# Top-k attention and two MLPs on one core: scores kept in PSUM, the mask on ScalarE, and another spread of the weight preparation

## The chip, the cores and the metric

The kernel runs on one core of one Trainium2 chip. The metric is the device time in microseconds (us) of one launch; lower is better. The engines are TensorE (PE, with its weight loads as PEld), VectorE (DVE), ScalarE (ACT), GpSimd (POOL) and SyncE (SP), which here issues all DMAs.

## What is computed

The reference chains an attention that keeps the 32 largest scores of each row and two MLPs of 512 x 2048 x 512 over 2304 tokens (4 batches x 576):

```python
scores = scale * np.matmul(q, k.transpose(0, 1, 3, 2))          # 4 batches, 8 heads, 576 x 576
kth = np.partition(scores, -32, axis=-1)[..., -32:-31]
scores = np.where(scores >= kth, scores, -1e9)
attn = softmax(scores)                                          # with 1e-9 in the denominator
x = np.matmul(attn, v)                                          # -> 2304 x 512
h = x @ w_in1;  g = where(h >= 1, h, where(h <= -1, 0, (h + 1) ** 2 / 4));  x = g @ w_out1
h = np.maximum(x @ w_in2, 0);  out = (h * h) @ w_out2
```

All arrays are float32. The kernel computes matrix products with pairs of float16: every operand is split into a high part and a low part (the rest), and three products (high x high, high x low, low x high) are added in PSUM.

## The kernel before

**Tiles and slots.** 2304 tokens are 18 token tiles of 128. One *tile* of the attention (number t, 144 in all) is one token tile and one head: 128 rows of 576 scores. Two of the token tiles, 4 and 13, straddle two batches; their scores and attends take twice as many matmuls of half the rows. One *MLP group* is a token tile and a quarter of the 2048 hidden columns, 12 matmuls for the input product and 12 for the output product, all 512 columns wide; there are 72 groups of each MLP, 144 in all.

**A tile of the attention.** PE makes the scores with four matmuls (512 and 64 columns, two parts) in a PSUM tile `s` (`scores`, L782). ACT copies them to an SBUF tile `S` (`scores_copy`, L795), of which there are five. DVE finds the 32 largest with four `max` (eight values each) and, between them, three `match_replace`, which overwrite the values found (`topk_ops`, L802); the first `max` and the first `match_replace` read `S`, the others the work tile `W`. A `match_replace` shows in the trace as two rows, MATCH_VALUE_LOAD and MATCH_REPLACE8. POOL makes the bias of the exponential (`exp_bias`), ACT takes the exponential of `S` (`exp`), DVE multiplies it with the comparison of `S` to the 32nd value (`mask`, a scalar_tensor_tensor). ACT writes the high part over `S` (`prob_hi`), POOL the low part in two pieces (`prob_lo`), SP issues a DMA transpose to `pT`, and PE multiplies with the values in 14 matmuls (`attend`, into `acc`).

**An MLP group.** PE fills `h` in PSUM (two banks). For the first MLP (`m == 1`) ACT makes two relus of `h` with different scales, POOL clamps the first (tensor_scalar to `r`), ACT squares it, POOL adds the second (tensor_tensor to `r`). For the second MLP ACT makes a relu and a square. ACT and POOL then split the result into `g`, SP transposes it to `gT`, and PE multiplies with the output weights into `o` (`mlp_act` to `mlp_out`). `y_finish` normalises the first MLP's result: its `hl_y<-o,sy,hl_y` on DVE reads PSUM.

**Weights.** The four weights come as float32, 16 slices of 128 x 512 each; they lie in the SBUF tile `wall`. `w_decode` (ACT, POOL and DVE, the last a scalar_tensor_tensor over 512 elements) brings the loaded words into a scaled form, `w_norm` sums squares on PE, `w_scale` makes a scale, and `w_split` (L512) makes high and low parts: for the first MLP with a float32 matmul by a diagonal, whose result ACT copies, for the second on ACT and POOL.

**The order.** Functions are noted at steps (eight steps are one slot of one tile) that the table `PLAN` sets. A planner, `Book.order`, puts the noted operations into one order per engine by a list schedule: every operation has a cost from `Book.costs`, an operation that is ready runs where its engine is free, the smaller key first. The engines then run that order as it stands. DVE's `max` operations form a beat; other operations may run at most 12 of them ahead.

Of the kernel before, what the change touches and what calls it, by code (L numbers as in the profile page):

```python
# [16 lines left out]
P = 128  # L17
# [4 lines left out]
TOPK = 32  # L22
# [13 lines left out]
    soon=dict(s=8, att=8, a=8, x=24),  # L36
    kch=(0, 0, 0, 1), vch=(0, 0, 1), scale=(0, 1, 2, 3, 4, 5), dch=(0, 1, 3), qch=(0, 0, 3, 4), k0=(-5, -4, -2),
    d0=(-8, -6, -4, -2), l0=(-9, -6), n0=(0, 1, 0, 1, 2, 3), q01=-5, v0l=-2, v0n=(5, 7, 9, 11), v0s=14, vn=60, vnd=7,
    vnl=18, vs=241, meet=248, mc1=252, m2c0=121, m2c1=265, v0=(21, 25, 29, 33, 37, 41, 45, 49), kv1=(254, 10, 289, 6),
# [107 lines left out]
class Book:  # L147
# [3 lines left out]
    def __init__(self, nc):  # L151
# [3 lines left out]
        self.shift = 0  # L155

    def tile(self, pool, bufs, shape, dtype, tag, name, given):
        ring = self.rings.get((id(pool), tag))
        if ring is None:
            ring = self.rings[id(pool), tag] = Ring(pool, bufs, dict(tag=tag, **given))  # L160
# [4 lines left out]
    def pool(self, real, bufs):  # L165
        book = self

        class Pool:
            def tile(self, shape, dtype, tag, name, **given):
                return book.tile(real, given.get("bufs", bufs), shape, dtype, tag, name, given)  # L170
# [12 lines left out]
    def note(self, engine, method, fn, args, kwargs):  # L183
# [7 lines left out]
        deps = set()  # L191
# [11 lines left out]
        for v in ins:  # L203
            c = v.cover()
            deps.update(n for d, n in v.tile.writes if meet(c, d))
            v.tile.reads.append((c, op.n))
        for v in outs:
# [14 lines left out]
            t.writes.append((c, op.n))  # L222
        op.load = method == "dma_start"
# [1120 lines left out]
```

## Time and profile before

| what | value |
|---|---|
| three runs, median | 1165.53 us (1162.1 to 1168.16) |
| profiled execution, its own time | 1160.56 us |
| its span, first to last instruction | 1158.8 us |
| busy: PE, DVE, ACT, POOL | 1000.6, 985.1, 855.3, 833.6 us |
| mean granted clock of PE | 0.975 |

All sums below are made against the profiled execution. The page of the profile gives busy shares; `out<-in` in a row names the tile that is written and those that are read. Nearly every row carries the line L339, since the planner emits all operations there, so rows are told apart by tile names: `m` holds the maxima, `s` and `S` scores, `W` the work tile and the probabilities, `r`, `g`, `h`, `o` belong to the MLP, `wall` to the weights. Matmuls are pipelined and their ends are modelled, so for PE the distance from start to start is the measure.

### The profile page before, as it was taken

Reading aid. Unit: us, or ns where it says so; the run is one execution under the profiler, and the core shown is the slowest. Engines: PE = TensorE matmul, PEld = TensorE weight load, DVE = VectorE, ACT = ScalarE, POOL = GpSimd, SP = SyncE. Lnnn points to the kernel's source line nnn. Section 1 sums busy time; section 2 is a strip of 40 time slices with the busy share of each in tenths; the row PEclk is TensorE's granted clock in tenths of the full one; section 3 lists DMA queues with packets and bytes.
Section 4 is the critical chain, followed back from the end, with each engine's and each line's share of the span. In section 5 each row is a group of like instructions: output and inputs, shape, how many; then the busy total and the mean of one; then the engine's idle time right before and its main releaser. Section 6 shows DMA issues by size and latency. Waiting matters only on the chain.

```text
span 1158.8 us, 20462 instructions
## 1 busy us (share of the span) xinstructions
PE 1000.6 (86%) x6700; PEld 483.2 (42%) x6700; DVE 985.1 (85%) x2039; ACT 855.3 (74%) x1613; POOL 833.6 (72%) x1148
## 2 busy tenths in 40 slices
PE   2347876778888999899998999999999998999997
PEld 1123432333344444444444444444444444444443
DVE  3989997998999999999999999999899999993000
ACT  5768988889667677877877777877767787766542
POOL 4784679999788785768896777778875757666431
PEclk9979987899999999999999999999999999999999
DMA  9977877675787677678876667769765666565332
GB/s 259 352 223 236 216 170 185 128 144 103 134 162 136 119 122 115 132 137 150 167 141 128 110 120 141 138 127 168 143 129 102 124 119 113 103 119 96 64 66 61
DMA packets 463387, 165.21 MB, mean 143 GB/s; under 512 B 441776, under 2 KB 448944, under 8 KB 463280
## 3 DMA queue, kind: packets, MB, share of 16 engines
q1 hardware_dynamic: 463280, 163.90, 68.7%
q8 instruction: 52, 0.85, 0.3%
q14 instruction: 55, 0.45, 0.1%
HBM read 55.31 MB, written 4.72 MB: 52 GB/s over the span
## 4 chain that ended last, share of the span: by engine, by line
DVE 28%; POOL 24%; PE 18%; DMA 12%; issue 8%; ACT 8%; SPq 1%; POOLq 0%; DVEq 0%; ACTq 0%
DVE W L339 14%; DVE m L339 11%; PE o L339 8%; PE h L339 8%; POOL wall L339 6%; POOL S L339 5%; DMA gT<-g 4%; POOL g L339 4%; POOL r L339 3%; ACT S L339 2%; DMA qT<-qhl 1%; ACT r L339 1%; SPq L339 1%; DMA wall<-in_moe_w_in_dram 1%; PE s L339 1%
## 5 line engine op out<-in xcount | busy, mean ns | idle before, releaser
L339 PE MATMUL o<-wall,gT 128*128 128x512 f16 x1728 | 425.2, 385 | 45.7 <-DMA gT<-g 42.9
L339 DVE MAX8 m<-W 128x8 f32<-128x576 f32 x432 | 322.7, 753 | 5.0
L339 PEld LDWEIGHTS <-gT 128*128 128x128 f16 x1728 | 160.8, 99 | 248.6 <-DMA gT<-g 69.0
L339 POOL TENSOR_TENSOR S<-W,S 128x64 f16<-128x64 f32 (+1 forms) x288 | 213.7, 760 | 69.5 <-ACT S L339 68.6
L339 POOL TENSOR_TENSOR g<-r,g 128x512 f16<-128x512 f32 x144 | 174.3, 1211 | 85.8 <-ACT g L339 65.5
L339 DVE MATCH_REPLACE8 W<-m,W 128x576 f32<-128x576 f32 x288 | 213.5, 741 | 0.0
L339 PE MATMUL h<-wall,T_x 128*128 128x512 f16 x864 | 207.3, 383 | 0.0
L339 PE MATMUL h<-wall,T_y 128*128 128x512 f16 x864 | 205.6, 379 | 1.0 <-ACT r L339 1.0
L339 ACT ACTIVATE W<-S,nb,esc 128x576 f32<-128x576 f32 x144 | 124.3, 863 | 38.8 <-DVE m L339 33.1
L339 DVE SCALAR_TENSOR_TENSOR W<-S,m,W 128x576 f32<-128x576 f32 x144 | 145.7, 1012 | 4.6 <-ACT W L339 4.5
L339 ACT ACTIVATE S<-W 128x576 f16<-128x576 f32 x144 | 98.3, 682 | 58.7 <-DVE W L339 54.6
L339 DVE MAX8 m<-S 128x8 f32<-128x576 f32 x144 | 107.7, 748 | 18.7 <-ACT S L339 18.6
L339 PE MATMUL s<-kst,qT 128*128 128x512 f16 (+3 forms) x640 | 103.9, 298 | 22.0 <-ACT S L339 18.7
L339 PEld LDWEIGHTS <-T_x 128*128 128x128 f16 x864 | 81.8, 99 | 93.2 <-issue 5.0
L339 PEld LDWEIGHTS <-T_y 128*128 128x128 f16 x864 | 81.3, 98 | 94.1 <-issue 2.6
L339 PE MATMUL acc<-vst,pT 128*128 128x65 f16 (+1 forms) x2240 | 100.8, 196 | 19.1 <-DMA pT<-S 9.7
L339 POOL TENSOR_TENSOR r<-r,g 128x512 f32<-128x512 f32 x72 | 93.8, 1302 | 21.5 <-ACT r L339 21.3
L339 PEld LDWEIGHTS <-pT 128*128 128x128 f16 (+1 forms) x2240 | 86.3, 102 | 54.5 <-DMA pT<-S 20.3
L339 ACT ACTIVATE g<-r 128x512 f16<-128x512 f32 x144 | 90.0, 625 | 24.1 <-POOL r L339 22.9
L339 DVE MATCH_REPLACE8 W<-m,S 128x576 f32<-128x576 f32 x144 | 106.9, 742 | 0.0
L339 ACT ACTIVATE S<-s 128x576 f32<-128x576 f32 x144 | 92.1, 640 | 12.0 <-PE s L339 11.9
L339 ACT ACTIVATE r<-r 128x512 f32<-128x512 f32 x144 | 90.5, 629 | 13.4 <-POOL r L339 11.5
(142 smaller groups left out, 1192.1 us busy)
## 6 DMA issues: line engine op xcount, KB each, us to landing
wall<-in_moe_w_in_dram SPq DMA_DIRECT2D x32, 512.0 KB, 6.5
wall<-in_moe_w_out_dram SPq DMA_DIRECT2D x30, 512.0 KB, 5.0
out_dram<-ob SPq DMA_DIRECT2D x18, 256.0 KB, 2.5
l_q<-in_q_dram SPq DMA_DIRECT2D x16, 256.0 KB, 3.7
n_v<-in_v_dram SPq DMA_DIRECT2D x24, 144.0 KB, 2.8
n_k<-in_k_dram SPq DMA_DIRECT2D x12, 288.0 KB, 3.0
l_k<-in_k_dram SPq DMA_DIRECT2D x12, 288.0 KB, 3.3
pT<-S SPq DMA_TRANSPOSE x144, 3.3
```

What stands on the lines that cost most here:

```text
L339: op.fn(*(real(a) for a in op.args), **{k: real(a) for k, a in op.kwargs.items()})
```

## The change

- **Scores stay in PSUM.** One PSUM tile `both` of three banks holds two tiles' scores: even tiles at columns 0 to 575, odd ones at 960 to 1535, so that the 64-column tails share the middle bank. The copy to `S` is gone; `max` and `match_replace` of a tile's first round read `both`. The bank of the weight norms is given up; they use a bank of `o`.
- **The mask moves to ACT.** POOL makes two biases after the last `max` (minus the 32nd value; the 32nd less the first, scaled). ACT takes a prelu of the scores less the 32nd value, whose slope of 2^97 sends all smaller scores far down (`below`), and then the exponential of that. The `mask` on DVE is gone. The four `W` and three float16 tiles `pc` replace the five `S`.
- **The first MLP's gate.** ACT makes relu, square, and a relu written back into `h`; DVE adds and clamps in one scalar_tensor_tensor that reads `h` in PSUM (`mlp_gate`). POOL's clamp and add are gone.
- **Weights.** A letter per slice says who makes its parts (`w_i1` and so on): P makes the high part on DVE and the low part with the matmul, D both on DVE, H scales and makes the high part on DVE and the low part on POOL, G, g and a spread the scaling over DVE, POOL and ACT. 22 slices go through the matmul instead of 32. In all DVE has 64 more tensor_scalars and 10 more scalar_tensor_tensors of 512 elements, and ACT makes 69 operations fewer.
- **First values.** Their three loads are noted later and depend on the second key transpose.
- **Planner.** Costs of `Book.costs` and steps of `PLAN` are changed, among them `odd=0` (the plain order of a tile's top-k), `N0=13` (MLP groups a slot later), `vn` and `vs` (the norms of later values), and `out` in `soon`.

```diff
-    soon=dict(s=8, att=8, a=8, x=24),
+    soon={'s': 8, 'att': 8, 'a': 8, 'x': 24, 'out': -4},
...
+        if method == "matmul":
+            p0, p1, at = outs[0].cover()[:3]
+            ends = outs[0].tile.ends
+            if kwargs["start"]:
+                deps.update(n for a, b, bank, n in ends if bank == at // 2048 and a < p1 and p0 < b)
...
+            if method == "tensor_scalar" and not any(v.tile.ring.psum for v in ins + outs):
+                n /= 2
+            c = 0.06 + n / 960 + (0.07 if method == "match_replace" else 0.25 if both > 1 else 0.06 if method != "max" else 0)
...
+            def high():
+                if how in "pP" and name not in diags:
+                    w_diag(name)
+                if how in "PD":
+                    DVE.tensor_scalar(hi, src, s, None, op0=ALU.mult)
+                else:
+                    ACT.activation(hi, src, AF.Copy, scale=s)
+
+        if how in "dD":
+            return [lambda: None, high, lambda: DVE.scalar_tensor_tensor(lo, src, s, hi, op0=ALU.mult, op1=ALU.subtract)]
...
+        def scale():
+            if how == "a":
+                ACT.activation(src, src, AF.Copy, scale=s)
+            elif how == "g":
+                POOL.tensor_scalar(src, src, s, 1.0, op0=ALU.mult, op1=ALU.mult)
             else:
+                DVE.tensor_scalar(src, src, s, None, op0=ALU.mult)
+
+        def high():
+            if how == "H":
+                DVE.tensor_scalar(hi, src, 1.0, None, op0=ALU.mult)
             else:
+                ACT.activation(hi, src, AF.Copy)
+
+        return [scale, high, lambda: POOL.tensor_tensor(lo, src, hi, op=ALU.subtract)]
...
+        book.hold = turned[PLAN["v0k"] : PLAN["v0k"] + 1]
         SP.dma_start(t[0:64, :, 0:256], src[:, :, 0:256])
         SP.dma_start(t[0:64, :, 256:320], src[:, :, 512:576])
         SP.dma_start(t[64:128], src[:, :, 256:576])
+        book.hold = ()
...
+    both = ps_s.tile([P, 1536], F32, tag="s", name="both")
+
     def scores(t):
         T, j = divmod(t, 8)
         d = st[t]
-        ps = ps_s.tile([P, 1024], F32, tag="s", name=f"s_{t}")
-        d["ps"] = ps
+        odd = t % 2
+        d["s"] = ps = both[:, 960 * odd : 960 * odd + S]
...
-    def scores_copy(t):
-        s = pool.tile([P, S], F32, tag="S", name=f"S_{t}", bufs=PLAN["sbufs"])
-        ACT.activation(s, st[t]["ps"][:, 0:S], AF.Copy)
-        st[t]["s"] = s
...
+        POOL.tensor_scalar(nb[:, 0:1], last, -1.0, 1.0, op0=ALU.mult, op1=ALU.mult)
+        POOL.tensor_scalar(nb[:, 1:2], last, d["m"][:, 0:1], d["esc"], op0=ALU.subtract, op1=ALU.mult)
+
+    def below(t):
...
+        ACT.activation(d["e"], d["s"], AF.Prelu, bias=d["nb"][:, 0:1], scale=1.0, alpha=2.0**97)
...
-    def mask(t):
-        d = st[t]
-        DVE.scalar_tensor_tensor(
-            d["e"],
...
         if m == 1:
-            u = g.rearrange("p a b -> p (a b)").bitcast(F32)
             ACT.activation(r, h, AF.Relu, bias=B1[:, column(T)], scale=A1[:, column(T)])
-            ACT.activation(u, h, AF.Relu, bias=NG[:, column(T)], scale=A2[:, column(T)])
-            POOL.tensor_scalar(r, r, RHO[:, column(T)], 0.0, op0=ALU.min, op1=ALU.max)
+            ACT.activation(r, r, AF.Square)
+            ACT.activation(h, h, AF.Relu, bias=NG[:, column(T)], scale=A2[:, column(T)])
...
     def mlp_gate(n):
         m, T, j = group(n)
+        r = rt[n]
         if m == 1:
-            POOL.tensor_tensor(rt[n], rt[n], gs[n].rearrange("p a b -> p (a b)").bitcast(F32), op=ALU.add)
+            h = hps[n].rearrange("p a b -> p (a b)")
+            DVE.scalar_tensor_tensor(r, h, G[:, column(T)], r, op0=ALU.add, op1=ALU.min)
```

What the planner makes of it, at three places. On DVE around tile 52 (the number in `m_52_...`; `rs`, `sc_y` are small operations of the finishing steps), before:

```order
L339 MAX m_52_5057<-S_5047 128x8
L339 MATCH_REPLACE W_5068<-m_52_5057,S_5047 128x576
L339 SCALAR_TENSOR_TENSOR W_4982<-S_4954,m_51_4973,W_4982 128x576
L339 MAX m_52_5057<-W_5068 128x8
L339 TENSOR_SCALAR rs_5087<-acc 128x1
L339 MATCH_REPLACE W_5068<-m_52_5057,W_5068 128x576
L339 MAX m_52_5057<-W_5068 128x8
L339 MATCH_REPLACE W_5068<-m_52_5057,W_5068 128x576
L339 MAX m_52_5057<-W_5068 128x8
L339 MAX m_53_5137<-S_5115 128x8
```

and with the change:

```order
L354 MAX m_52_4883<-both 128x8
L354 MAX m_51_4821<-W_4831 128x8
L354 MATCH_REPLACE W_4909<-m_52_4883,both 128x576
L354 MAX m_52_4883<-W_4909 128x8
L354 TENSOR_SCALAR rs_4931<-acc 128x1
L354 MATCH_REPLACE W_4909<-m_52_4883,W_4909 128x576
L354 MAX m_52_4883<-W_4909 128x8
L354 MATCH_REPLACE W_4909<-m_52_4883,W_4909 128x576
L354 MAX m_53_4973<-both 128x8
L354 MAX m_52_4883<-W_4909 128x8
```

The mask of tile 51 is gone from the middle of tile 52, whose operations now mostly stand directly behind one another; the scores are read from `both`, and a tile's last `max` stands behind the next tile's first.

On ACT, a stretch with a group of the first MLP (`r`, `g`, `h` with the operands A and B) and one tile, before:

```order
L339 ACTIVATE r_5255<-h_5206,B_785,A_819 128x512
L339 ACTIVATE g_5263<-h_5206,NG,A_825 128x512
L339 ACTIVATE S_5275<-s_5258 128x576
L339 ACTIVATE r_5255<-r_5255 128x512
L339 ACTIVATE W_5223<-S_5198,nb_5228,esc_4327 128x576
```

and with the change:

```order
L354 ACTIVATE r_5364<-h_5318,B_722,A_796 128x512
L354 ACTIVATE r_5364<-r_5364 128x512
L354 ACTIVATE h_5318<-h_5318,NG,A_807 128x512
L354 ACTIVATE W_5300<-both,nb_5396 128x576
L354 ACTIVATE W_5300<-W_5300,nb_5396,esc_4865 128x576
L354 ACTIVATE g_5425<-r_5364 128x512
L354 ACTIVATE pc_5430<-W_5300 128x576
```

The copy `S<-s` is gone; a prelu out of `both` stands ahead of the exponential, and the second relu goes back into `h`.

On SP at the start, before (the rows ahead are loads of queries, keys and weights):

```order
L339 DMA wall<-in_v_dram 64x8x256
L339 DMA wall<-in_v_dram 64x8x64
L339 DMA wall<-in_v_dram 64x8x320
L339 DMA_TRANSPOSE qT_0_155<-qhl_0_131 128x8x128
L339 DMA_TRANSPOSE kst_0_179<-wall 128x9x128
L339 DMA_TRANSPOSE kst_1_191<-wall 128x9x128
```

and with the change:

```order
L354 DMA_TRANSPOSE qT_0_152<-qhl_0_122 128x8x128
L354 DMA_TRANSPOSE kst_0_163<-wall 128x9x128
L354 DMA_TRANSPOSE kst_1_178<-wall 128x9x128
L354 DMA_TRANSPOSE kst_2_187<-wall 128x9x128
L354 DMA_TRANSPOSE kst_3_199<-wall 128x9x128
L354 DMA_TRANSPOSE qT_1_215<-qhl_1_195 128x8x128
L354 DMA wall<-in_v_dram 64x8x256
```

The three loads of the first values now stand behind the transposes of queries and keys.

## Rows read from the trace of the kernel before

**Rows 1.** Busy times by stretch: us, then each engine's busy us (instructions), clock, DMA share.
```profile
0.00:400.00 400.00, 284.80 (x1926) 138.11 (x1927) 356.26 (x756) 312.64 (x614) 315.79 (x429) 0.93 0.78 185
400.00:1000.00 600.00, 565.82 (x3931) 275.19 (x3929) 572.87 (x1169) 457.25 (x854) 442.41 (x629) 1.00 0.70 130
1060.00:1159.00 99.00, 91.95 (x449) 41.43 (x445) 3.09 (x12) 41.51 (x70) 33.61 (x36) 0.99 0.34 68
```

**Rows 2.** Waits of DVE, 400 to 1000 us: in total, times, longest.
```profile
DVE m L339 <- ACT S L339: 9.3, 15, 2.0
```

**Rows 3.** Tile S, 400 to 1000 us: min/median/max ns, first and last start.
```profile
L339 DVE MAX8 m<-S x90: 728/744/762, 401.8 to 995.6; 128x8 f32<-128x576 f32 x90
```

**Rows 4.** Timeline of PE at two places: start us, length us, operation, count.
```profile
603.27 0.65 PE L339 MATMUL s<-kst,qT 128*128 128x512 f16 x4
603.76 1.46 PE L339 MATMUL o<-wall,gT 128*128 128x512 f16 x6
605.06 0.60 PE L339 MATMUL acc<-vst,pT 128*128 128x65 f16 x14
605.49 0.81 PE L339 MATMUL o<-wall,gT 128*128 128x512 f16 x3
...
1084.10 1.67 PE L339 MATMUL h<-wall,T_x 128*128 128x512 f16 x7
...
1089.28 1.67 PE L339 MATMUL h<-wall,T_x 128*128 128x512 f16 x7
```

**Rows 5.** Groups of DVE by shape, 400 to 1000 us: busy us, mean ns | idle before.
```profile
L339 DVE SCALAR_TENSOR_TENSOR W<-S,m,W 128x576 f32<-128x576 f32 x90 | 90.5, 1005 | 3.3 <-ACT W L339 3.3
...
L339 DVE SCALAR_TENSOR_TENSOR hl_y<-o,sy,hl_y 128x512 f16<-128x512 f32 x12 | 8.9, 742 | 0.0
```

**Rows 6.** Timeline of DVE, 603 to 606 us.
```profile
603.48 0.76 DVE L339 MAX8 m<-W 128x8 f32<-128x576 f32 x1
604.27 0.09 DVE L339 MATCH_VALUE_LOAD W<-m,W 128x8 f32 x1
604.35 0.74 DVE L339 MATCH_REPLACE8 W<-m,W 128x576 f32<-128x576 f32 x1
605.13 0.76 DVE L339 MAX8 m<-W 128x8 f32<-128x576 f32 x1
605.80 0.74 DVE L339 MAX8 m<-S 128x8 f32<-128x576 f32 x1
```

**Rows 7.** Groups by shape, the whole program.
```profile
L339 DVE SCALAR_TENSOR_TENSOR W<-S,m,W 128x576 f32<-128x576 f32 x144 | 145.7, 1012 | 4.6 <-ACT W L339 4.5
L339 ACT ACTIVATE W<-S,nb,esc 128x576 f32<-128x576 f32 x144 | 124.3, 863 | 38.8 <-DVE m L339 33.1 <-POOL qhl L339 3.3 <-DVE sy L339 0.6
...
L339 ACT ACTIVATE S<-W 128x576 f16<-128x576 f32 x144 | 98.3, 682 | 58.7 <-DVE W L339 54.6 <-DVE mc L339 3.4
L339 POOL TENSOR_TENSOR r<-r,g 128x512 f32<-128x512 f32 x72 | 93.8, 1302 | 21.5 <-ACT r L339 21.3
L339 ACT ACTIVATE S<-s 128x576 f32<-128x576 f32 x144 | 92.1, 640 | 12.0 <-PE s L339 11.9
...
L339 POOL TENSOR_SCALAR nb<-m,esc 128x1 f32<-128x1 f32 x144 | 53.5, 371 | 43.2 <-DVE m L339 32.4 <-DVE sq L339 5.2 <-DVE A L339 1.8
L339 POOL TENSOR_SCALAR r<-r,RHO 128x512 f32<-128x512 f32 x72 | 51.2, 711 | 20.6 <-ACT r L339 20.3
...
L339 DVE SCALAR_TENSOR_TENSOR wall<-wall 128x512 int32<-128x512 int32 x62 | 48.7, 787 | 6.8 <-POOL wall L339 4.8 <-issue 1.4 <-ACT wall L339 0.5
...
L339 DVE TENSOR_SCALAR neg<-ident 128x128 f16<-128x128 bf16 x1 | 0.2, 195 | 0.0
```

**Rows 8.** The start: chain of waits, timeline of DVE, DMA issues (us to landing).
```profile
19.19 5.43 DMA kst<-wall
...
26.50 0.76 DVE L339 MAX8 m<-S 128x8 f32<-128x576 f32 x1 [5.88 <-ACT S L339]
...
pT<-S SPq DMA_TRANSPOSE x144, 3.3
```

More of the change, by code (lines that the diff above doesn't have):

```diff
@@ L155, in __init__, with tile @@
         self.shift = 0
-    def tile(self, pool, bufs, shape, dtype, tag, name, given):
+        self.hold = ()
+    def tile(self, pool, bufs, shape, dtype, tag, name, given, psum):
         ring = self.rings.get((id(pool), tag))
         if ring is None:
-            ring = self.rings[id(pool), tag] = Ring(pool, bufs, dict(tag=tag, **given))
+            ring = self.rings[id(pool), tag] = Ring(pool, bufs, dict(tag=tag, **given), psum)
         self.names += 1
@@ L204, in note @@
             c = v.cover()
-            deps.update(n for d, n in v.tile.writes if meet(c, d))
+            before = [n for d, n in v.tile.writes if meet(c, d)]
+            assert before, (method, v.tile.name)
+            deps.update(before)
             v.tile.reads.append((c, op.n))
@@ L242, in costs @@
             a = args[1].tile.dtype
-            c = max(n * (4 if a is F32 else 1) / 2370.0, 0.044)
+            c = max(n * (4 if a is F32 else 1) / 2370.0, 0.03)
             return c, c + 0.2
+        both = sum(not v.tile.ring.psum for v in ins if v.elements() > 64)
         if engine == "DVE":
@@ L393, in scale_from_norm2 @@
         ]
-    bank = ps_j.tile([P, P], F32, tag="gram", name="bank")
     ident = cpool.tile([P, P], BF16, tag="ident", name="ident")
@@ L519, in w_split @@
+        if how in "pP":
             ps = []
-            def high():
-                if c == 0 or c == 8 and len(set(DIAG_AT[name])) == 2:
-                    DVE.tensor_scalar(diag, ident, s, None, op0=ALU.mult)
-                ACT.activation(hi, src, AF.Copy, scale=s)
             def low():
                 ps.append(ps_h.tile([P, 4, P], F32, tag="h", name=f"lo_{name}_{c}").rearrange("p a b -> p (a b)"))
-                PE.matmul(ps[0], diag, src, start=True, stop=False)
+                PE.matmul(ps[0], diags[name], src, start=True, stop=False)
@@ L739, in exp_scale @@
                 )
+            POOL.tensor_scalar(esc, esc, 2.0**-56, 1.0, op0=ALU.max, op1=ALU.mult)
             ld["esc", T] = esc
@@ L818, in exp_bias @@
         d = st[t]
[L819 to L820 removed]
+        nb = small.tile([P, 2], F32, tag="nb", name=f"nb_{t}", bufs=4)
+        last = d["m"][:, TOPK - 1 : TOPK]
         d["nb"] = nb
+        if t in PLAN["md"]:
+            POOL.tensor_scalar(nb[:, 1:2], d["m"][:, 0:1], d["esc"], -1.0, op0=ALU.mult, op1=ALU.mult)
+            return
+        POOL.tensor_scalar(nb[:, 0:1], last, -1.0, 1.0, op0=ALU.mult, op1=ALU.mult)
@@ new lines, in prob_hi @@
+        if t in PLAN["phd"]:
+            DVE.tensor_scalar(d["hi"], d["e"], 1.0, None, op0=ALU.mult)
+        else:
+            ACT.activation(d["hi"], d["e"], AF.Copy)
+    def prob_lo(t):
+        p, pc, hi = st[t]["e"], st[t]["pc"], st[t]["hi"]
+        at, tail = (64, 0) if t % 2 else (0, 512)
+        to = 0 if t % 2 else S
+        POOL.tensor_tensor(pc[:, to : to + 64], p[:, tail : tail + 64], hi[:, tail : tail + 64], op=ALU.subtract)
+        POOL.tensor_tensor(pc[:, S + 64 :], p[:, at : at + 512], hi[:, at : at + 512], op=ALU.subtract)
@@ L1285, in tile_topk_attention_mlp_mlp @@
     for s in range(NSLOT):
-        for fn, key in ((scores, "scores"), (scores_copy, "copy"), (exp, "exp"), (exp_bias, "bias"), (prob_hi, "phi"),
+        for fn, key in ((scores, "scores"), (exp_bias, "bias"), (below_, "below"), (exp, "exp"), (prob_hi, "phi"),
                         (prob_lo, "plo"), (prob_trans, "ptr"), (attend, "att")):
```

158 lines of the change are left out of this document (77 added, 81 removed), and 6 rows, old and new, of the table ORDERS.

## Prediction

> **What bounds the kernel now.** I read the busy times by stretch first [rows 1]. From 400 to 1000 us VectorE (DVE) is busy for 572.87 of 600 us and TensorE (PE) for 565.82, ScalarE (ACT) and GpSimd (POOL) for three quarters. In the first 400 us DVE is again the fullest, 356.26 us; in the last 99 us it has nothing left, and PE works off the MLP groups that trail the attention by about sixteen.
>
> Who waits for whom separates the two full engines. In the 600 us the largest wait of DVE is 9.3 us [rows 2]. So DVE runs without a break and sets the pace: 90 tiles start between 401.8 and 995.6 us [rows 3], 593.8 / 89 = 6.67 us a tile.
>
> PE is not far behind, and its busy time hides how far, so I worked out its floor from starts of matmuls [rows 4]. In the tail 24 matmuls of 512 columns recur every 1089.28 - 1084.10 = 5.18 us, one MLP group. A tile's four score matmuls take 603.76 - 603.27 = 0.49 us until the next matmul starts, its 14 attend matmuls 605.49 - 605.06 = 0.43. Floor: 5.18 + 0.49 + 0.43 = 6.10 us a tile. At best PE lets 0.57 us a tile be gained.
>
> **The steady stage, tiles 46 to 143.** The change takes the mask off DVE: 90.5 us in 90 tiles [rows 5]. It adds the gate of the first MLP, a scalar-tensor-tensor over 512 elements with one operand in PSUM; the same form exists, hl_y<-o,sy,hl_y, at 742 ns [rows 5]. One tile in two has one: 45 x 0.742 = 33.4 us.
>
> The third term is not in the diff. The order of DVE puts a tile's operations directly behind each other much more often: between the first max of tile 46 and that of tile 136 a max is directly followed by its own match_replace 195 times (139 before), a match_replace by its own max 171 times (109 before), 118 more pairs. Such a follower starts late [rows 6]: max to its own value load 604.27 - 603.48 = 0.79 us, against 605.80 - 605.13 = 0.67 when an unrelated max follows. A match_replace's own max starts 605.13 - 604.35 = 0.78 after it, as late for an operation of the same length, so I price both kinds of pair alike: 118 x 0.12 = 14 us come back. Net: -90.5 + 33.4 + 14 = -43 us on 600, or 6.19 us a tile.
>
> Reading scores from PSUM instead of SBUF has no row for max or match_replace. The nearest on DVE is again hl_y with an operand in PSUM: 742 ns, beside 787 for the decode's form with the same 512 elements and both operands in SBUF [rows 7]: PSUM is not dearer there, so I take zero. From below, ACT copies 576 elements out of PSUM in 640 ns and out of SBUF in 682 [rows 7], -0.04 us. From above, hl_y takes as long as a match_replace with 64 elements more [rows 5, 6]; at 742 / 576 = 1.3 ns an element that is +0.08. With two readers a tile on DVE the bounds are -7 and +14 us over 90 tiles.
>
> [...]
>
> DVE at 6.19 and PE at its floor of 6.10 are now the same length, and both run in a fixed order. The five SBUF score buffers are gone: a score buffer is free again only after the whole top-k of its tile, the bias on POOL and the prelu on ACT. I let mutual waiting eat 20 of the 43 us (ends: none, and all). Left: 23 in 90 tiles, 0.26 us a tile, **25 us** over 98 tiles.
>
> What is laid on ACT and POOL I cost at nothing here. ACT: a copy out of PSUM of 640 ns becomes a prelu with one pointer operand, between 640 and the 863 of the exp with two [rows 7]; take 0.75, +0.11 us a tile on an engine with 143 us free in 600. Its cover is that free time; without it the price is 0.11 x 98 = 11 us. Prelu runs already in the weight decode, between exps, so it brings no function that ACT does not switch to now. POOL loses the clamp (51.2 us) and the add (93.8 us) of the first MLP and gains a second one-column bias of 371 ns a tile, 144 x 0.371 = 53 us [rows 7]: 92 us less in the program. The h bank is held longer (three ACT passes and the gate), but the second bank covers it: an MLP group recurs every 6 us and a hold is three ACT passes, each under the exp's 0.86, and the gate: under 3.4, plus queues.
>
> **The first 400 us, tiles 0 to 45.** DVE loses 46 masks, (145.7 - 90.5) / 54 = 1.02 us each, 47 us [rows 5, 7]. It gains 16 gates, 12 us; 64 tensor_scalars that scale or make high parts, and 10 low parts at the decode's 787 ns, 8 us. A 512-wide tensor_scalar of f32 has no row: below stands the 128-wide one at 195 ns, above the two-operand 787 ns [rows 7]. I take 0.45, since one operand is read and its fixed part is in the 195: 64 x 0.45 = 29 us (13 to 50). Sum for DVE: -47 + 12 + 29 + 8 = +2 us, so no gain on the engine that is fullest there. ACT loses 69 passes over a weight slice, at some 0.68 us (the copy from SBUF [rows 7]) 47 us; POOL loses 16 clamps and adds, 32 us, against 17 us of biases. That only shortens waits of DVE, which is idle 44 us in the 400 [rows 1]; I take 4.
>
> At the start the value loads move behind the key transposes on SP's queue. The first key transpose takes 5.43 us from 19.19 to landing, where one of the same shape takes 3.3 in the median [rows 8], and DVE waits 5.88 us for the first scores, which also lose the ACT copy of 0.64. I take 2 us; the values land later, but no attend is needed before the first MLP group's input. Early gain: **6 us** (0 to 15, or a loss of 15 with a dear tensor_scalar).
>
> **The tail.** In the order 17 MLP groups follow the last attend instead of 16. PE alone works there: **+5 us**.
>
> **Sum.** -25 - 6 + 5 = -26 us against the profiled execution's own 1160.6: 1134.6. The median of the three runs, 1165.5, lies 4.9 above that execution, so I forecast **1139**.
>
> **Rivals.** *No mutual waiting* (0.12): DVE gets its 43 us whole (47 over 98 tiles) and ACT's and POOL's relief brings 15 early: 1160.6 - 47 - 15 + 5 = 1104, median 1108. For it: PE's order has the groups where they were relative to the tiles. Against it: two engines of equal length have never run without waits in this trace; PE stands idle for 34 us of the 600 now [rows 1].
>
> *The ring of two score buffers stalls DVE* (0.14), slower. From the last max of tile t to the first max of tile t + 2 run a bias (0.37), the prelu (0.75) and the four matmuls (0.65): 1.8 us with empty queues. Meanwhile DVE has the rest of tile t + 1, some 4 us of its 4 x 0.79 + 3 x 0.87 = 5.8 [rows 6]. In front of each step may stand a POOL subtract of 1.2, an ACT pass of 0.8 and a block of 12 matmuls, 2.6: then it is 6.4 us, and DVE stands still for over 2. The forecast holds 0.22 us of waiting a tile; the gain is gone at 0.22 + 26 / 144 = 0.40 us. At 0.6 us a tile: 1139 + 0.38 x 98 + 10 early = 1186. For it: the five buffers that hid such delays are gone. Against it: POOL is relieved.
>
> *Every reader in PSUM pays the upper bound on DVE* (0.08): 288 x 0.08 = 23 us; PE's wait takes some of that up, about two thirds count: 1139 + 15 = 1154. For it: hl_y against match_replace [rows 5, 6]. Against it: hl_y against the decode [rows 5, 7]. [...]
>
> *A wash* (0.08): DVE's freed time turns into waits for PE, whose order is no shorter, and the tail takes the rest: 1160 to 1170.
>
> **How the numbers follow.** The forecast has 0.58, with a range of its own of 1120 to 1156. The 80% range reaches into the stronger gain and into the milder half of the stall: 1106 to 1176. Faster by over 0.5%, which is what a measurement of this kernel can tell from no change, means under 1159.7: forecast, stronger gain and the dearer readers, 0.78. Within: the wash, 0.08. Slower: 0.14.
>
> **What would show it.** The profile after should have some 6.4 us from first max to first max, DVE and PE both at 95% or more from 400 to 1000 us, max and match_replace at about 750 ns out of PSUM, gates near 742, high parts near 0.45 us, DVE's work before tile 46 unchanged. It is wrong if DVE waits for PE's scores or for ACT by more than 0.4 us a tile, if the first max out of PSUM takes over 0.85 us, or if tile 46 starts later than the 401.8 us of before.

## The result, and the profile after

The changed kernel takes **1150.32 us** (median of 4 runs, 1149.5 to 1152.42) against 1163.84 (1162.1 to 1168.16) of the kernel before, timed beside it: ratio 0.9881, 95% interval 0.9847 to 0.9915. It is faster by 13.5 us, half of the 26 that I forecast, and inside the forecast's own range of 1120 to 1156. The profiled execution took 1149.5 us, its span is 1147.7: 11.1 less than the 1158.8 of before.

The page of the changed kernel, part 1 (busy):

```profile
PE 986.0 (86%) x6670; PEld 477.4 (42%) x6670; DVE 962.2 (84%) x2041; ACT 831.1 (72%) x1544; POOL 710.9 (62%) x1161
```

The same by stretch of time:

```profile
core 0: us, PE busy (x) PEld busy (x) DVE busy (x) ACT busy (x) POOL busy (x), PEclk, DMA share, GB/s
0.00:100.00 100.00, 37.31 (x254) 19.64 (x255) 78.43 (x169) 59.50 (x114) 68.87 (x116) 1.00 0.87 248
100.00:200.00 100.00, 55.93 (x397) 28.80 (x397) 95.07 (x184) 62.76 (x118) 85.82 (x99) 0.80 0.79 204
200.00:300.00 100.00, 80.60 (x497) 37.65 (x497) 97.35 (x216) 76.73 (x172) 67.18 (x96) 0.93 0.64 134
300.00:400.00 100.00, 90.17 (x709) 43.33 (x709) 96.60 (x225) 73.86 (x128) 67.16 (x127) 0.98 0.76 138
400.00:1000.00 600.00, 582.52 (x4057) 283.38 (x4055) 554.25 (x1167) 481.70 (x882) 373.86 (x660) 1.00 0.73 136
```

Against [rows 1], the two full engines have changed places from 400 us on: PE has 582.52 of 600, DVE only 554.25. In the first 400 us DVE is fuller than before, 78.43 + 95.07 + 97.35 + 96.60 = 367.5 us against 356.3, and works on the same tiles. Up to the first max of tile 46 itself (before, then changed):

```profile
0.00:401.80 401.80, 286.60 (x1940) 138.99 (x1941) 358.06 (x761) 314.40 (x617) 316.58 (x430) 0.93 0.78 184
```

```profile
0.00:405.00 405.00, 269.01 (x1894) 131.96 (x1895) 372.32 (x801) 276.27 (x538) 291.07 (x440) 0.93 0.77 181
```

DVE is busy 14.3 us longer there and idle 11.0 less (32.7 for 43.7), which leaves the stage 3.2 longer.

The first max of each tile marks the stages. The rows of the first max on DVE, from the start to tile 46 and from there to tile 143 (durations as minimum/median/maximum in ns, then first and last start):

```profile
L354 DVE MAX8 m<-both x47: 729/754/767, 24.8 to 405.0; 128x8 f32<-128x576 f32 x47
...
L354 DVE MAX8 m<-both x98: 745/752/768, 405.0 to 1029.1; 128x8 f32<-128x576 f32 x98
```

The span splits at these marks into three stages, and their sum is the whole difference (the marks of before are its first maxes, of which [rows 3] shows tile 46):

| stage | before | after | change | forecast |
|---|---|---|---|---|
| start to tile 46 | 401.8 | 405.0 | +3.2 | -6 |
| tile 46 to 143 | 645.0 | 624.1 | -20.9 | -25 |
| tile 143 to the end | 112.0 | 118.6 | +6.6 | +5 |
| span | 1158.8 | 1147.7 | -11.1 | -26 |

So the steady stage is nearly as forecast, and the early stage, where I expected a gain, lost. Of the missing 15 us the early stage is 9, the steady one 4 and the tail 2.

What is waited for from 400 to 1000 us has turned round as well. DVE's largest waits, in the chain of waits of the changed kernel (total, times, longest):

```profile
DVE W L354 <- ACT W L354: 14.3, 16, 1.4
DVE m L354 <- PE both L354: 13.3, 18, 2.5
```

Before, its largest was 9.3 us in all, for the copy of the scores [rows 2]; now it waits 27.6 us for these two, half for PE's scores, half for ACT's passes over `W`. PE is idle for 17.5 of the 600 us, and nearly all of that is one wait, for the transposes of `g` ahead of the output matmuls:

```profile
PE o L354 <- DMA gT<-g: 16.0, 18, 2.6
```

In the early stage, these groups of DVE are new or changed (from 0 to 402 us; count, then busy time and mean in ns):

```profile
L354 DVE SCALAR_TENSOR_TENSOR wall<-wall 128x512 int32<-128x512 int32 x62 | 55.1, 890 | 4.5 <-POOL wall L354 4.4
...
L354 DVE TENSOR_SCALAR wall<-wall,s_i 128x512 f16<-128x512 f32 x21 | 13.5, 644 | 0.1
L354 DVE SCALAR_TENSOR_TENSOR r<-h,G,r 128x512 f32<-128x512 f32 x16 | 11.8, 739 | 0.0
L354 DVE TENSOR_SCALAR wall<-wall,s_o 128x512 f32<-128x512 f32 x16 | 11.4, 712 | 0.0
L354 DVE TENSOR_SCALAR wall<-wall 128x512 f16<-128x512 f32 x14 | 7.5, 535 | 0.0
...
L354 DVE TENSOR_SCALAR wall<-wall,s_o 128x512 f16<-128x512 f32 x11 | 6.5, 588 | 0.0
L354 DVE SCALAR_TENSOR_TENSOR wall<-wall,s_o 128x512 f16<-128x512 f32 x7 | 6.4, 913 | 0.0
...
L354 DVE SCALAR_TENSOR_TENSOR wall<-wall,s_i 128x512 f16<-128x512 f32 x3 | 3.6, 1215 | 0.0
...
L354 DVE TENSOR_SCALAR wall<-wall,s_i 128x512 f32<-128x512 f32 x2 | 2.2, 1082 | 0.0
```

The 64 tensor_scalars take 13.5 + 11.4 + 7.5 + 6.5 + 2.2 = 41.1 us (29 forecast), the ten low parts 10.0 (8 forecast), and the 62 decodes, which the change does not touch, 55.1 where they took 48.7 [rows 7].

### The profile page after: what moved, and what is told of

Its sections match the earlier page's. It is cut to its first block, busy times and chain, and to the rows that moved or that the text cites. A ratio compares the mean times of both kernels' runs of the same rounds, so it can differ in the third digit from the quotient of the medians.

```text
span 1147.7 us, 20648 instructions
## 1 busy us (share of the span) xinstructions
PE 986.0 (86%) x6670; PEld 477.4 (42%) x6670; DVE 962.2 (84%) x2041; ACT 831.1 (72%) x1544; POOL 710.9 (62%) x1161
## 4 chain that ended last, share of the span: by engine, by line
PE 26%; DVE 12%; issue 5%; DMA 5%; ACT 4%; POOL 2%; SPq 1%; POOLq 0%; ACTq 0%; DVEq 0%
PE o L354 12%; PE h L354 11%; DVE m L354 5%; DVE W L354 5%; DMA gT<-g 4%; ACT W L354 2%; PE both L354 2%; PE acc L354 1%; POOL pc L354 1%; POOL g L354 1%; SPq L354 1%; DVE r L354 1%; ACT pc L354 1%; DMA qT<-qhl 0%; POOL nb L354 0%
## 5 line engine op out<-in xcount | busy, mean ns | idle before, releaser
L354 PE MATMUL o<-wall,gT 128*128 128x512 f16 x1728 | 435.8, 382 | 23.9 <-DMA gT<-g 23.5
L354 DVE MAX8 m<-W 128x8 f32<-128x576 f32 x432 | 325.8, 757 | 7.0
L354 POOL TENSOR_TENSOR g<-r,g 128x512 f16<-128x512 f32 x144 | 168.7, 1172 | 203.3 <-ACT g L354 170.9
L354 PEld LDWEIGHTS <-gT 128*128 128x128 f16 x1728 | 162.4, 98 | 228.3 <-DMA gT<-g 40.9
L354 POOL TENSOR_TENSOR pc<-W,pc 128x64 f16<-128x64 f32 (+1 forms) x288 | 209.0, 746 | 71.4 <-ACT pc L354 65.6
L354 DVE MATCH_REPLACE8 W<-m,W 128x576 f32<-128x576 f32 x288 | 213.7, 742 | 0.0
L354 PE MATMUL h<-wall,T_x 128*128 128x512 f16 x864 | 209.2, 383 | 1.3 <-ACT wall L354 0.7
L354 PE MATMUL h<-wall,T_y 128*128 128x512 f16 x864 | 207.7, 379 | 1.7 <-ACT r L354 1.2
L354 ACT ACTIVATE W<-both,nb 128x576 f32<-128x576 f32 x144 | 106.4, 740 | 118.8 <-DVE W L354 50.1
L354 PE MATMUL both<-kst,qT 128*128 128x64 f16 (+3 forms) x640 | 101.8, 300 | 45.2 <-ACT W L354 28.6
L354 ACT ACTIVATE W<-W,nb,esc 128x576 f32<-128x576 f32 x144 | 124.1, 862 | 11.1 <-POOL nb L354 7.1
L354 DVE MAX8 m<-both 128x8 f32<-128x576 f32 x144 | 108.7, 755 | 24.8 <-PE both L354 19.6
L354 PEld LDWEIGHTS <-T_x 128*128 128x128 f16 x864 | 82.1, 99 | 98.0 <-issue 9.3
L354 PEld LDWEIGHTS <-T_y 128*128 128x128 f16 x864 | 81.5, 98 | 93.4 <-issue 2.3
L354 PEld LDWEIGHTS <-pT 128*128 128x128 f16 (+1 forms) x2240 | 91.0, 102 | 43.9 <-issue 15.4
L354 DVE MATCH_REPLACE8 W<-m,both 128x576 f32<-128x576 f32 x144 | 107.6, 748 | 0.0
L354 ACT ACTIVATE g<-r 128x512 f16<-128x512 f32 x144 | 90.0, 625 | 19.9 <-DVE r L354 18.8
L354 PE MATMUL acc<-vst,pT 128*128 128x65 f16 (+1 forms) x2240 | 98.5, 196 | 2.1 <-ACT x L354 1.0
L354 ACT ACTIVATE pc<-W 128x576 f16<-128x576 f32 x144 | 97.4, 676 | 1.0
L354 ACT ACTIVATE r<-r 128x512 f32<-128x512 f32 x144 | 90.3, 627 | 2.6
L354 DVE SCALAR_TENSOR_TENSOR r<-h,G,r 128x512 f32<-128x512 f32 x72 | 53.4, 742 | 41.9 <-ACT h L354 41.9
L354 POOL TENSOR_SCALAR nb<-m 128x1 f32<-128x1 f32 x144 | 31.8, 221 | 85.2 <-DVE m L354 66.5
```

The lines of the kernel that those rows point to most:

```text
L354: op.fn(*(real(a) for a in op.args), **{k: real(a) for k, a in op.kwargs.items()})
```

## The experiments

Twelve kernels ran. My theory after the result had two parts: the early stage was lost to weight work on a DVE that is full there, and from some 300 us on PE sets the pace. (From 300 to 400 us DVE is still the fuller, 96.60 against 90.17; what is tested below is the stage from 400 us on.) Each run was timed beside the kernel before, whose median was 1163.8 to 1165.2 each time, so medians of different rows compare to about 1.5 us; its profile gives tile 46 and the stages.

| run | median us | ratio, 95% interval | tile 46 | tile 46 to 143 |
|---|---|---|---|---|
| the change | 1150.3 | 0.9881 (0.9847 to 0.9915) | 405.0 | 624.1 |
| weights_back | 1142.7 | 0.9802 (0.9774 to 0.9829) | 394.7 | 626.6 |
| weights_half | 1134.1 | 0.9753 (0.9729 to 0.9777) | 388.6 | 624.8 |
| values_back | 1142.0 | 0.9799 (0.9773 to 0.9825) | 403.6 | 618.9 |
| both_back | 1154.8 | 0.9907 (0.9885 to 0.9928) | 397.3 | 632.5 |
| shuffle_both | 1152.2 | 0.9911 (0.9882 to 0.9941) | 402.0 | 626.0 |
| shuffle_sp | 1149.5 | 0.9880 (0.9855 to 0.9905) | 404.7 | 622.3 |
| shuffle_pe | 1155.3 | 0.9930 (0.9902 to 0.9958) | 409.3 | 625.0 |
| n12 | 1153.5 | 0.9887 (0.9853 to 0.9921) | 404.5 | 634.7 |
| pe_light | 1138.7 | 0.9773 (0.9752 to 0.9795) | 411.9 | 610.6 |
| nogate | 1144.3 | 0.9821 (0.9803 to 0.9838) | 399.7 | 623.4 |
| mask_back | 1203.8 | 1.0328 (1.0299 to 1.0356) | 438.6 | 654.8 |
| before_plain | 1175.9 | 1.0092 (1.0070 to 1.0114) | 409.4 | 652.4 |

### Which engine paces the steady stage: nogate and pe_light

```diff
-            DVE.scalar_tensor_tensor(r, h, G[:, column(T)], r, op0=ALU.add, op1=ALU.min)
+            pass
```

> The changed kernel without the scalar_tensor_tensor that adds and clamps the first MLP's activation (DVE has 72 x 0.742 = 53 us less, 12 us of it before tile 46; r goes on unclamped). Theory (PE paces from 300 us on): the 12 us help early, the rest goes into idle time of DVE: 1138 to 1150, tiles 46 to 136 at 6.3 to 6.43 us. Rival (DVE paces): 0.37 us a tile less in the steady stage and 12 early: 1100 to 1110.

Tile 46 comes 5.3 us earlier, of the 12 that I expected; the steady stage takes 623.4 instead of 624.1, the time falls by 6. Taking 0.37 us a tile off DVE there gives nothing; DVE waits instead. In its chain of waits from 400 to 1000 us:

```profile
DVE m L354 <- PE both L354: 23.9, 19, 10.7
DVE W L354 <- ACT W L354: 19.0, 22, 1.1
```

These are 42.9 us where the change has 27.6. The rival, that DVE paces, falls.

```diff
-        PE.matmul(o, g[:, 0, fb, :], w_lo(w, c, 0, 512), start=False, stop=False)
+        if fb:
+            PE.matmul(o, g[:, 0, fb, :], w_lo(w, c, 0, 512), start=False, stop=False)
```

> The changed kernel with one of the 24 matmuls of an MLP group left out (high x low of the first of four column blocks of the output product): PE has 0.216 us a group less, 31 us in 144 groups, at the 216 ns from start to start of a 512-column matmul. Theory: since the change PE paces the kernel from about 300 us on (97% busy, 6.25 us of PE time a tile), so nearly all of it is won where groups run behind each other: 20 to 31 us, 1119 to 1130. Rival: DVE still paces, or the mutual waiting: the 17 groups of the tail give 3.7 us and the steady stage at most 10: 1136 to 1147.

The steady stage falls by 13.5 us, of the 97 x 0.216 = 21 taken out, and the tail by 4.2 to 114.4; but tile 46 comes 6.9 later, in an order that the planner made anew. The time fell by 11.6, short of the 20 to 31 and inside the rival's 1136 to 1147; what speaks against the rival is the steady stage, 13.5 where it has 10 at most. The order alone can move more than that difference (the shuffles below), so this run by itself does not exclude mutual waiting. With nogate, and with a PE that is busy for 582.52 and waits for transposes for 16.0 of 600 us, PE is what mainly paces the steady stage, but not alone: only two thirds of what is taken from PE comes back, and its idle time grows from 17.5 to 26.7 us. In both runs PE has the fuller row from 400 to 1000 us, pe_light the less full of the two (nogate first, then pe_light):

```profile
400.00:1000.00 600.00, 581.57 (x4050) 284.55 (x4048) 529.77 (x1117) 485.56 (x882) 376.60 (x664) 0.99 0.73 135
```

```profile
400.00:1000.00 600.00, 573.26 (x4035) 279.94 (x4034) 559.63 (x1187) 484.79 (x896) 383.42 (x680) 1.00 0.75 137
```

### The mask alone: mask_back

```diff
-scores=-6, below=8, wbufs=4, md=(), exp=9, ...
+scores=-6, below=8, wbufs=4, md=tuple(range(144)), exp=9, ...
```

> The changed kernel with the mask on DVE again for all 144 tiles: ACT's prelu and POOL's second bias are gone, ACT takes the exponential of the scores in PSUM, DVE multiplies with the comparison; all else (scores in PSUM, gate on DVE, weights) as in the changed kernel. My theory: DVE is still the engine that paces, with PE close behind, so 1.0 us a tile comes back early (46 us) and, in the steady stage, what DVE then has more than today's 6.43 us a tile: 6.16 busy + 1.0 + waits of 0.1 to 0.3, some 7.3 us a tile, +0.87 x 98 = 85 us: 1260 to 1290. Rival 1: what the steady stage waits for today is not DVE, and the mask would fill idle time: less than +40 us. Rival 2: the two score buffers, held until the mask, stall DVE: DVE waits for PE's scores by over 1 us a tile, 1300 or more.

It costs 53.5 us, less than half of what I expected and more than the first rival's 40: 33.6 before tile 46 and 30.7 in the steady stage, with 10.6 back in the tail. Three premises were wrong. DVE did not pace the changed kernel, so a little of the mask goes into its waits. The mask is not 1.0 us any more. And a row's length is not what the operation adds to DVE's busy time. The stretch from 400 to 1000 us of mask_back:

```profile
400.00:1000.00 600.00, 562.95 (x3893) 272.51 (x3892) 562.42 (x1197) 401.33 (x749) 337.41 (x549) 1.00 0.71 129
```

A tile takes (1048.3 - 438.6) / 90 = 6.77 us in it, so DVE is busy for 562.42 / 600 x 6.77 = 6.35 us a tile, where the changed kernel has 554.25 / 600 x 6.43 = 5.94. That is 0.41 more, and 0.07 less waiting. Neighbouring rows overlap (in the changed kernel a max of 0.76 us starts at 606.71 and the next one at 607.38), and an operation between a max and its own match_replace takes up the wait of that pair (there a max starts at 610.53, a one-column tensor_scalar at 611.21 and the max's own value load at 611.33, 0.80 after the max, as with nothing between); how much of the mask's 0.81 us is either was not measured. The mask's rows over the whole program, first of the kernel before, then of mask_back:

```profile
L339 DVE SCALAR_TENSOR_TENSOR W<-S,m,W x144: 798/810/1804, 37.5 to 1054.2; 128x576 f32<-128x576 f32 x144
```

```profile
L354 DVE SCALAR_TENSOR_TENSOR W<-both,m,W x144: 793/809/819, 35.8 to 1102.3; 128x576 f32<-128x576 f32 x144
```

The median is the same; the mean of 1012 ns [rows 7] came from a tail up to 1804 that is gone when the scores are read from PSUM. (1012 - 809) x 144 = 29 us of the mask stand above the mean of mask_back, which has the mask still on DVE and the scores in PSUM. It is not that POOL has less work in mask_back: 50 of its masks lie for over 80% of their time under a POOL instruction and take 807 ns in the mean, where the 75 such masks of the kernel before take 1052 and the 39 with less than 20% take 806. The second rival (stalls for the two score buffers) falls too: in this run DVE waits for PE's scores only 2.3 us between 400 and 1000 us.

### The early stage: weights_back, weights_half

```diff
-    w_i1="PPPPPPPPgagPgaga", w_o1="PHPHPHPHgHgHgHgH", w_i2="DHDHDPPPPPPPPgPg", w_o2="DHDHgHDGDGDGDGDH",
+    w_i1="pppppppppppppppp", w_o1="ppppppppagagagag", w_i2="agagagagagagagag", w_o2="agagagagagagagag",
```

> The changed kernel with the weight spread of before: all high parts on ACT, 24 slices' low parts by the matmul and ACT's copy, the rest scaled on ACT and POOL in turn with POOL's subtract; DVE makes no weight part. My theory: the early stage missed its forecast because the high and low parts on DVE cost 51 us there (41.1 for 64 tensor_scalars, 10.0 for ten scalar_tensor_tensors), 14 more than I summed, on the engine that is 95% busy from 100 to 400 us. Without them DVE has 51 us less before tile 46 and ACT some 45 more; ACT has the room (59 to 77 of each 100 us), so tile 46 starts 10 to 35 us before 405 and the time is 1115 to 1140. Rival 1: the spread is a gain all the same, because ACT and POOL would be the later link of the decode and of the first weights: tile 46 at 405 or later, time 1150 to 1170. Rival 2: the early loss is of the later value norms or of the two score buffers: time within 4 us of 1150.

Here 24 slices go through the matmul; in the kernel before it was 32. Tile 46 starts at 394.7, 10.3 us earlier, and the time falls by 7.6: the direction of the theory, at the low end of its range. 51 us off DVE bought only 10. The windows of weights_back show why:

```profile
100.00:200.00 100.00, 71.25 (x454) 35.38 (x455) 85.23 (x169) 87.54 (x169) 75.37 (x99) 0.82 0.84 212
200.00:300.00 100.00, 77.70 (x490) 35.90 (x489) 78.62 (x178) 87.32 (x187) 85.57 (x122) 0.85 0.62 128
```

DVE is no longer full (78.62 of 100), while ACT rose from 76.73 to 87.32 and POOL from 67.18 to 85.57 between 200 and 300 us: DVE now waits. Before tile 46 it is busy for 332.69 us and idle for 62.0, where the changed kernel has 32.7, and the largest wait from 0 to 400 us is for PE's scores (changed kernel first, then weights_back):

```profile
DVE m L354 <- PE both L354: 6.3, 5, 2.6
```

```profile
DVE m L354 <- PE both L354: 22.6, 11, 8.7
```

That asks for the middle, a kernel with only the 22 high parts of the matmul slices on ACT:

```diff
-    w_i1="PPPPPPPPgagPgaga", w_o1="PHPHPHPHgHgHgHgH", w_i2="DHDHDPPPPPPPPgPg", w_o2="DHDHgHDGDGDGDGDH",
+    w_i1="ppppppppgagpgaga", w_o1="pHpHpHpHgHgHgHgH", w_i2="DHDHDppppppppgpg", w_o2="DHDHgHDGDGDGDGDH",
```

> The changed kernel with the high parts of the 22 slices that go through the matmul on ACT instead of DVE (22 x 0.64 = 14 us of DVE's work before tile 46 moved; the other 42 tensor_scalars and the ten scalar_tensor_tensors stay). Theory, the work on DVE before tile 46 is what delays it: a good quarter of the 51 us that gave 10 us in weights_back, so tile 46 some 3 us before 405 and 1142 to 1150, within what the order does. Rival, the high part's place matters more than its length, since the low part's matmul and ACT's copy hang on it: tile 46 at 395 or earlier, or later than 405.

I expected a quarter of the gain of weights_back and got more than all of it: tile 46 at 388.6 and **1134.1 us**, the fastest of all versions, 16 us under the change and 30 under the kernel before. Its windows:

```profile
100.00:200.00 100.00, 64.05 (x411) 32.54 (x410) 96.78 (x192) 72.42 (x141) 91.22 (x109) 0.74 0.82 210
200.00:300.00 100.00, 83.17 (x559) 39.78 (x557) 97.18 (x209) 83.03 (x180) 64.52 (x95) 0.93 0.69 138
```

DVE is still full, and up to tile 46 its busy time is less by about what was moved:

```profile
0.00:388.60 388.60, 268.69 (x1897) 133.16 (x1898) 358.14 (x780) 287.48 (x560) 288.83 (x440) 0.92 0.80 189
```

That is 14.2 us less busy and 2.2 less idle. Tile 46 before 395 is what the rival had foretold, by the place of the high part in the chain of PE and ACT; but a chain that comes sooner would show in DVE's waits, and they make 2.2 of the 16.4. So here each microsecond taken off the full engine counted about once, within what the order alone moves (next section), and what is won at tile 46 reaches the end: the time fell by 16.2. It is no rate to rely on. nogate took 11.8 us of gates off the same stage and won 5.3: DVE's busy time to tile 46 fell by only 7.7, to 364.65 us, and its idle time rose by 2.4. The gain of weights_back is smaller because it takes off 51 and DVE then waits. That ACT and POOL, fuller there, are what makes PE's scores late is argued, not shown. My expectation had scaled linearly between the two ends, where a point between them is better than both.

### The order itself: the two shuffles

```diff
-        return 1.32, n * 256 / 1000 / 165
+        return 1.34, n * 256 / 1000 / 165
```

> A null: the changed kernel with one constant of the planner's cost for a DMA transpose at 1.34 instead of 1.32. No work, wait or step is added or taken; only the order that the list schedule makes comes out otherwise in places (184 of DVE's 1600 rows stand elsewhere). If the fate of the order is worth nothing, the time stays within 2 us of 1150. Theory: it is worth several us, since both engines run in fixed orders near full: 1140 to 1158, with tile 46 within 3 us of 405 and the difference in the steady stage.

```diff
-            return c, c + 0.2
+            return c, c + 0.21
```

> A second null: the changed kernel with the planner's latency of a matmul at 0.21 instead of 0.20. Same work, another order (578 of DVE's 1600 rows stand elsewhere). As for the first null: within 2 us of 1150 if the order does not matter, 1140 to 1158 by my theory, tile 46 within 3 us of 405.

The first moves nothing (-0.8 us), the second costs 4.9, of which 4.3 stand at tile 46 already, more than I had allowed, and not in the steady stage where I had looked for it. Two draws do not make a distribution, but they say that a difference of 5 us between two planned orders needs no other cause.

### The values' steps: values_back, both_back, shuffle_both

```diff
-... v0l=0, v0k=1, ... vn=112, vnd=6, vnl=18, vs=276, meet=283, mc1=287, m2c0=121, m2c1=300 ...
+... v0l=-2, v0k=9, ... vn=60, vnd=7, vnl=18, vs=241, meet=248, mc1=252, m2c0=121, m2c1=265 ...
```

(With `v0k=9` the three loads wait for no transpose.)

> The changed kernel with the value loads of the first batch at their old step and without the wait for the key transpose, and with the norms and scales of the later values at their old steps (60 and 241 instead of 112 and 276). My theory (dear weight parts on DVE): this does not move the early loss, tile 15 starts within 5 us of 170.3 and the time is within 4 us of 1150; the first max comes some 2 us later. Rival: the order of the values made the early loss: tile 15 starts 8 us earlier or more, time 1140 to 1146.

Tile 15 stays late (171.8 against 170.3), as the theory wanted, so the values are not the early loss. But the time fell by 8.4, to what the rival had named without its sign at tile 15, and 5.2 of it lie in the steady stage, where neither had looked. The wait for the transposes itself shows where it should and dies out: tile 2 starts at 36.9 with it and at 41.3 without, tile 5 at 62.8 and 61.5.

> The changed kernel with both: the weight spread of before (as in weights_back, 1142.7) and the order of the values of before (as in values_back, 1142.0). Theory A, the two losses are separate (weight parts load DVE before tile 46; the value steps move 5 us in the steady stage): the gains add, 1150.3 - 7.6 - 8.4 = 1134, with tile 46 near 393. Theory B, what values_back won is the luck of another order in the planner, since it won nothing before tile 46 beyond 1.4 us: 1139 to 1146.

> The weight spread and the value steps of before (both_back, 1154.8) with the first null's planner constant, 1.34. If both_back was slow only by the order it fell into, this comes out anywhere from 1135 to 1150, and tile 46 stays some 7 us or more ahead of 405. If the two edits really stand against each other, it stays at 1152 to 1157.

Both put weights and values back. Neither theory of both_back held: it is slower than either edit alone. Its reshuffle stays in the range that I had named for two edits that stand against each other. In both, tile 46 is ahead of 405 (397.3 and 402.0), as with the weights alone, but less so, and the steady gain of values_back is absent. Whether values_back was a lucky order or the two edits really conflict is not settled.

### The tail: n12

```diff
-spd_o2=8, mc0=55, N0=13, early=0,
+spd_o2=8, mc0=55, N0=12, early=0,
```

> The changed kernel with the MLP groups one slot earlier (N0 = 12), so that 16 groups follow the last attend, not 17. My tail term says one group of 5.2 us less: 1145. Rival 1: the slot only moves the group into the early stage, where PE is idle anyway but the first weights come no sooner, and the groups end as late: within 2 us of 1150. Rival 2: groups that run earlier in the order make DVE and PE wait for the weights: slower, 1153 or more.

The tail is 5.6 us shorter (1152.3 - 1039.3 = 113.0), as the term said, and the steady stage 10.6 longer. A group of 5.2 us that PE does before the last tile instead of after it only pushes the tiles back, if PE is full; the other 5 us are of the size of the shuffles. The time is also that of the second rival, but tile 46 is no later than 405 and among the waits of 1.3 us or more from 400 to 460 us PE has none for weights. The term was sized right; that it was no cost rests on this one run.

### The pairs on DVE: before_plain

```diff
-        (((0, 0),), ((1, 4),), ((0, 1),), ((2, 7),), ((0, 2),), ((1, 5),), ((0, 3),), ((1, 6),)),
+        (((0, 0),), ((0, 1),), ((0, 2),), ((1, 7),), ((0, 3),), ((0, 4),), ((0, 5),), ((0, 6),)),
```

with `odd=0`. The mask is noted here ahead of the exponential that it should follow, so the exponential overwrites it and the output is unmasked.

> The kernel before with the plain order of the top-k (a tile's operations behind each other, the mask of the tile before between them), all else as it was: in DVE's order 413 pairs of a max and a match_replace of the same tile stand directly behind each other, 318 before, 95 more. My term of 0.12 us a pair, on the engine that paces this kernel: +11 us, about 1176. Rival 1: the pairs cost nothing, because the engine's gap overlaps: within 3 us of 1165. Rival 2: the plain order frees buffers sooner and is a gain: under 1160.

The time, 1175.9, is the expected one, but the mask and the exponential have also exchanged their waits, and 7.6 of the 11 us stand before tile 46. It does not decide. The price of a pair is read better from the changed kernel's timeline of DVE (start, duration):

```profile
605.17 0.76 DVE L354 MAX8 m<-W 128x8 f32<-128x576 f32 x1
605.97 0.09 DVE L354 MATCH_VALUE_LOAD W<-m,W 128x8 f32 x1
...
606.71 0.76 DVE L354 MAX8 m<-both 128x8 f32<-128x576 f32 x1
607.38 0.74 DVE L354 MAX8 m<-W 128x8 f32<-128x576 f32 x1
```

A max is followed by its own value load after 605.97 - 605.17 = 0.80 us, by another tile's max after 607.38 - 606.71 = 0.67. Over the whole program a value load starts 0.80 us after the max ahead of it in the median of 258 such neighbours, and a max 0.68 after another max in the median of 111. What the 118 pairs cost in all no run isolates.

## Why the prediction was half right

**Right, and shown.**
- *The mask's removal and what it is worth in the steady stage*: -20.9 us from tile 46 to 143 against -25. Between 46 and 136 a tile takes (983.6 - 405.0) / 90 = 6.43 us (6.4 forecast). DVE's busy time fell from 572.87 / 600 x 6.67 = 6.37 to 5.94 us a tile, 0.43 of the 0.48 in my sum.
- *The gate at 742 ns* out of PSUM: 739 early, 743 in the median of all 72.
- *The surcharge of a score in PSUM as zero*: the first max takes 755 ns in the mean against 748, the first match_replace 748 against 742, +5 to +7 ns each (before, then changed):

  ```profile
  L339 DVE MAX8 m<-S 128x8 f32<-128x576 f32 x144 | 107.7, 748 | 18.7 <-ACT S L339 18.6
  L339 DVE MATCH_REPLACE8 W<-m,S 128x576 f32<-128x576 f32 x144 | 106.9, 742 | 0.0
  ```

  ```profile
  L354 DVE MAX8 m<-both 128x8 f32<-128x576 f32 x144 | 108.7, 755 | 24.8 <-PE both L354 19.6 <-ACT W L354 2.6 <-ACT pc L354 1.7
  L354 DVE MATCH_REPLACE8 W<-m,both 128x576 f32<-128x576 f32 x144 | 107.6, 748 | 0.0
  ```

  Over the whole program that is 288 x 0.0065 = 2 us, not the 288 x 0.08 = 23 of the rival of dear readers, which falls.
- *The prelu at 0.75 us*: 740 ns in the mean, and the exponential behind it is as long as before, 862 ns against 863. Either trace has one ACT_TABLE_LOAD, of 1.28 us at the start, so the prelu brings none.
- *The pair price of 0.12 us*: 0.80 against 0.67.
- *The ring of two score buffers does not stall DVE*: 13.3 us of waits for PE's scores in 600, no 0.4 us a tile. The rival on the slower side is out.

**Wrong.**
- *"I take 0.45 ... 64 x 0.45 = 29 us" and "So no gain on the engine that is fullest there"*, the step that failed. A tensor_scalar of 512 elements cost 0.64 in the mean, a low part 1.0 instead of 0.787, and a decode that the change does not touch 0.89 instead of 0.787. With these the sum for DVE before tile 46 is -47 masks + 11.8 gates + 41.1 + 10.0 + 6.4 = +22 us, not +2, and its measured busy time there grew by 14.3 (neighbouring rows overlap, and its small operations took 4 us less). weights_half shows what that is worth: 14 of these us moved off give 16.
- *"Early gain: 6 us"* follows from it: a loss of 3.2. The 6 are 4 us of shorter waits and 2 at the start, where the first max did come 1.7 earlier (24.8 for the 26.5 of [rows 8]); the +2 of my own sum for DVE is left out of them. DVE's idle time before tile 46 did shrink, by 11.0 us, more than the 6, but 14.3 us more work ate it. The run with the 22 high parts on ACT says that ACT had room which the change left unused.
- *"I let mutual waiting eat 20 of the 43 us"*: the amount was about right (DVE's idle time grew from 0.30 to 0.49 us a tile, 17 us in 90 tiles), but 20 was a guess between none and all, so that is luck, and the picture was wrong. What mainly holds the steady stage is PE: its busy time is 582.52 / 600 x 6.43 = 6.24 us a tile, 0.14 above the floor of 6.10 that I had put together from three spacings, which left out the tiles across two batches with twice the matmuls, among others. The same reading of [rows 1] gives 565.82 / 600 x 6.67 = 6.29 for the kernel before. nogate shows that DVE had time to spare.
- *"PE alone works there: +5 us"*: the tail did grow by 6.6, but n12, one run, won nothing by shortening it, with PE full before it.

What I had named as signs would have told: tile 46 later than 401.8, and high parts far from 0.45.

## What to carry to other kernels

When work is spread anew over engines, look at each stretch for the engine that is full there and move only as much as the next one has free: here 14 us off the full engine won 16, and 51 us won 10 (one run each). Take the pace of a stage from the busy time per tile of that stage, not from a floor built of single spacings, and try it by making one engine lighter at a time. Where a planner makes the order anew from its costs, run one or two null changes of it first: here they moved the time by up to 5 us, and terms below that cannot be told apart by one run.

## What the runs showed of the hardware that I had not expected

The weight operations of DVE, which read and write SBUF alone, have a long tail of durations in a stretch where GpSimd is busy too (68.87, 85.82 and 67.18 us of the first three 100 us); the gate and hl_y, with one operand in PSUM, have none. The rows of the changed kernel over the whole program:

```profile
L354 DVE SCALAR_TENSOR_TENSOR wall<-wall x62: 655/694/2186, 10.7 to 217.8; 128x512 int32<-128x512 int32 x62
...
L354 DVE TENSOR_SCALAR wall<-wall x14: 401/414/981, 133.5 to 291.5; 128x512 f16<-128x512 f32 x14
```

```profile
L354 DVE SCALAR_TENSOR_TENSOR r<-h,G,r x72: 721/743/752, 165.0 to 1095.5; 128x512 f32<-128x512 f32 x72
```

The gate never takes over 752 ns, hl_y never over 753, and the mask never over 819 once its scores are in PSUM (above). Max and match_replace out of `W`, in SBUF alone as well, have no tail either (at most 762 and 754 ns), so operands in SBUF are not enough for one. Sorted by how much of each lay under a POOL instruction in the trace, the 43 weight tensor_scalars with more than 80% took 650 ns in the mean, the 12 in between 755, the 9 with less than 20% took 449, about the 0.45 of my sum. The gates do not divide so: 741 ns for the 19 with more than 80%, 743 for the 43 with less than 20%. The sorting rests on POOL's spans in the trace and the middle group is the slowest, so this is a correlation and not a measurement of POOL's part. Why the weight operations have the tail (up to 2186 and 981 ns) and the gate has none (752) no run here shows. No run here held POOL idle during the weight work, so the share of it in the 41.1 us is not measured.
